# Regrouping the tiled matmuls of a fused attention and gating layer: v pairs and head sums in five clusters, a fourth product buffer, and two output groups in one sequence

## The chip, the cores and the metric

The kernel runs on one core of a Trainium2 chip. The core has five engines, each with its own in-order stream of instructions: TensorE (PE in the profile; its weight loads are listed as PEld), VectorE (DVE), ScalarE (ACT), GpSimd (POOL) and SyncE (SP), and they wait for each other through semaphores. Matrix products go to an accumulator memory (PSUM) of eight banks, and VectorE or ScalarE carries them on from there. DMA queues are issued from SP, ACT and POOL. The metric is the device time of one execution in microseconds (us), the median of the runs taken.

## What is computed

From one input x (2048 tokens, 512 features) a layer norm is taken, and two branches work on it; the output is x plus both.

```python
xn = _layernorm(x)
# attention: 32 heads of 16, each token looks at itself and 7 earlier ones, 2 apart
qkv = xn @ wqkv
logits = einsum('bhsd,bhswd->bhsw', q, k_gathered) * 16 ** -0.5      # w = 0..7
o = einsum('bhsw,bhswd->bhsd', softmax(logits), v_gathered)
att = o @ wo
# gating: F = 1376, two halves of 688
z = gelu(xn @ w_in)
z1, z2 = z[..., :688], layernorm(z[..., 688:])
g = einsum('ts,bsf->btf', w_sp, z2) + b_sp
out = x + att + (z1 * g) @ w_out
```

All inputs and the output are in bfloat16; sums are kept in float32.

## The kernel before

The 2048 tokens are 16 tiles of 128, and for attention two halves (`th`) of 1024. Two hand-written lists set the order. `ten` is the order of the steps that hang on TensorE, `vec` of those that hang on VectorE. Every step has a short name; `needs` says which steps must have been written down before it, and `advance` writes both lists out into one program, in which each engine keeps its own order. What waits at run time follows from the data: a step waits until what it reads is there and what it overwrites has been read.

The steps that matter here:

- `z`*i* and `h`*i*: the second half of w_in for token tile *i* (eight full matmuls, L203), and its gelu on ScalarE (L209); `q`*i*: the sum of squares on ScalarE (L214). `zs`*i*: the mean and variance for four tiles, three small VectorE operations (L220 to L222) and the root on GpSimd (L223, L224). `zn`*i*: the normalisation of one tile on VectorE (L230), which waits for that root.
- `y`*i*: the first half of w_in for a tile (L203 again, gelu L235). `k`*b c*: q or k for 512 tokens, two chunks of features (L243, copied by ScalarE, L245).
- `v`*n*: a "v pair", v for two of the 16 places in a head (L258). Its matmuls use a quarter of the array's columns each, at tile positions (0, 0) to (0, 96), four side by side.
- `m`*th w*: the products of q and k for two window places on VectorE (L278, two operations of 128x4096), into one of the product buffers. Their features are added up in two folds, the first on VectorE (`f`, L281) or by an accumulating DMA from the GpSimd queue (`d`, L287), the second on VectorE (`p`, L282).
- `S`*th w*: the head sum (L293), four column-tiled matmuls against a matrix of ones, and the scaled copy of the result by ScalarE into `a_sb` (L295). It needs `p`*th w*.
- `M`*j*: a tile of the token mixing (L362, 32 full matmuls), which reads all of z2, so that its *k*-th pair of matmuls needs `zn`*k*. `g`*j*: the gate on VectorE (L370) and the transposes of the result. `x`, `e`, `u`, `i`, `c`: the softmax. `a`*th.n*: the weighted sum of v on VectorE (L335, L339, L348).
- `B`: a small transpose of the bias on TensorE (L576). `W`, `O`, `X`: loads. `O` loads wo and w_out over the weights that were there.
- `Q`*n*: an output group of four token tiles: attention @ wo (L412, row-tiled, four matmuls of 32 rows side by side), the full feature blocks of the gating branch (L400) and its remainder of 48 rows (L406, two side by side). `F`*n* adds the residual on VectorE (L417) and stores.

A product buffer is a "home". Before, there are three: two tiles of their own, and the first part of the buffer of z1. `home` gives the home of each of the eight products; a product that takes a home again waits for the head sum that read it last.

PSUM is held in three tiles of two banks (`mm`) and two of one bank (`aux`), each taken in turn. In the output stage all eight banks are dealt out to the groups (`banks`, `po`).

Three sizes of matmul tile occur in the regrouped part: 128*128 (full), 128*32 (v pairs, head sums) and, in the output groups, 64*128 for the remainder (48 rows in use) and 32*128 for attention. The source calls going from one to another a change of kind. Output groups 0 and 1 before: full, remainder, attention, then attention, remainder, full.

Of the kernel before, what the change touches and what calls it, by code (L numbers as in the profile page):

```python
# [14 lines left out]
S = 2048  # L15
D = 512
NT = S // P
# [21 lines left out]
def kernel(  # L39
# [45 lines left out]
    xnT = xnT_r[:].rearrange("p (c s) -> p c s", c=C)  # L85
    op = xnT_r[:].rearrange("p (t d s) -> p t d s", t=2, d=DH)
    wts = sb.tile([P, C * (3 * D + F)], BF16, name="wts")
    w_q, w_k, w_v = [wts[:, n * C * D:(n + 1) * C * D].rearrange("p (k f) -> p k f", k=C) for n in range(3)]
    w_z = [wts[:, C * (3 * D + n * FH):C * (3 * D + (n + 1) * FH)].rearrange("p (k f) -> p k f", k=C) for n in range(2)]
    wo_r = wts[:, 0:DH * D].rearrange("p (d n) -> p d n", d=DH)  # L90
    wout = wts[:, DH * D:(DH + MF + 1) * D].rearrange("p (m n) -> p m n", m=MF + 1)
    qk_r = [sb.tile([P, QKH], BF16, name=f"qk{t}") for t in range(2)]
# [7 lines left out]
    z1_r = sb.tile([P, NT * FP], BF16, name="z1")  # L100
    z1u = z1_r[:].rearrange("p (i f) -> p i f", i=NT)
    prod.append(z1_r[:, 0:2 * C * HS])
    xs = z1_r[:, 0:NT * D].rearrange("p (i d) -> p i d", i=NT)
    xn = [z1_r[:, NT * D + n * D:NT * D + (n + 1) * D] for n in range(8)]
    vp = sb.tile([P, DH, 2, HALO + GS], BF16, name="vp")
# [8 lines left out]
    def nxt(kind, pool):  # L114
        t = pool[count[kind] % len(pool)]
        count[kind] += 1
        return t
# [145 lines left out]
        G.dma_start(vp[H:P, :, :, 0:HALO], vp[0:P - H, :, :, GS:GS + HALO])  # L263
        G.dma_start(vp[0:H, :, 1, 0:HALO], vp[P - H:P, :, 0, GS:GS + HALO])

    home = {(0, 0): 0, (0, 1): 1, (0, 2): 2, (0, 3): 0, (1, 0): 1, (1, 1): 0, (1, 2): 1, (1, 3): 0}

    def prod_ops(th, w2):
        pr = prod[home[th, w2]].rearrange("p (w c s) -> p w c s", w=2, c=C)
# [18 lines left out]

    def head_sum(th, w2):
        pr = prod[home[th, w2]].rearrange("p (w c s) -> p w c s", w=2, c=C)  # L290
        pl = nxt("aux", aux)
        for g in range(4):
            PE.matmul(pl[32 * g:32 * g + 32, :], rsel[:], pr[:, :, 0, g * GS:(g + 1) * GS],  # L293
                      start=True, stop=True, tile_position=(0, 32 * g))
        A.activation(a_sb[:, th, 2 * w2:2 * w2 + 2, :], pl[:].rearrange("p (w s) -> p w s", w=2),  # L295
                     ACT.Copy, scale=float(DH) ** -0.5)

    def softmax_max(th):
# [125 lines left out]
    for i in range(5, NT):  # L424
# [1 line left out]
    front += " n15 t15"  # L426
    vec = front.split() + """
        zs0 LW m00 j00 zn0 zn1 zn2 zn3 f00 p00 K m01 d01 m02 d02 zs4 m03 d03 zn4 zn5 zn6 zn7
        zs8 p01 p02 zn8 zn9 zn10 zn11 m10 p03 W1 f10 zs12 p10 zn12 zn13 zn14 zn15
        m11 d11 g0 x0 m12 d12 p11 g1 u0 m13 p12 W2 W3 f13 p13 c0 g2  # L430
        a0.0 a0.1 g3 x1 a0.2 a0.3 g4 a0.4 g5 a0.5 a0.6 a0.7 g6 u1 a0.8 g7 a0.9 g8 a0.10 g9 a0.11 c1 g10
        a1.0 a1.1 g11 a1.2 a1.3 g12 a1.4 g13 a1.5 g14 a1.6 a1.7 g15 a1.8 a1.9 F0 a1.10 a1.11 F1 F2
    """.split()
    ten = """
        T0 T1 GL z0 z1 h0 T3 h1 z2 h2 z3 h3 k00 k01 q0 k02 k03 q1 q2 q3 k10 k12 k11 k13
        W0 k20 z4 h4 q4 k21 z5 h5 q5 k22 z6 h6 q6 k23 z7 h7 q7 k30 z8 h8 q8 k31 z9 h9 q9 S00
        k32 z10 h10 q10 k33 z11 h11 q11 z12 h12 z13 h13 q12 v0 q13 v1 S01 S02 z14 h14 z15 h15 q14 v2 q15 v3 B
        y0 v4 S03 y1 M0 S10 v5 v6 EL v7 H e0 M1 EG y2 S11 y3 y4 EL1 i0 EG1 M2 y5 y6 y7 y8 S12 S13 M3 y9 y10 y11 M4 y12
        M5 W4 W5 y13 y14 y15 EL2 e1 M6 M7 W6 i1 M8 M9 W7 M10 O4 M11 O0 M12 O1 M13 O2 M14 O3 X0 M15 X1 Q0 Q1 Q2 Q3
    """.split()  # L440
    prods = [n for n in vec if n[0] == "m"]

    def needs(n):
        k, a = n[0], n[1:]
        i = int(a) if a.isdigit() else 0
        if k == "T":
            return [f"n{i}"]
        if k == "z" and a.isdigit():
            return [[f"T{i}"], ["T1", "n2"], ["z1"], ["T3"]][i] if i < 4 else [f"t{i}"]
        if n == "GL":  # L450
            return ["T1"]
        if k == "q":
            return [f"h{i}"]
        if k == "h":
            return [f"z{i}"]
        if k == "k":
            last = 4 * int(a[0]) + 3
            return [f"T{last}" if last < 4 else f"t{last}"]
        if k == "v":
            return ["t15", "LW"]  # L460
        if k == "S":
            return ["p" + a]
        if k == "m":
            b = 2 * int(a[0])
            r = ([f"k{x}3" for x in (b, b + 1)] + ["K"]) if b else ["k03", "k12"] + (["k13"] if a != "00" else [])
            prev = [p for p in prods[:prods.index(n)] if home[int(p[1]), int(p[2])] == home[int(a[0]), int(a[1])]]
            return r + (["S" + prev[-1][1:]] if prev else [])
        if k == "j":
            return ["k13"]
        if k in "fdp":  # L470
            return ["m" + a]
        if k == "K":
            return ["k13"]
        if n[:2] == "zs":
            return [f"q{int(n[2:]) + x}" for x in range(4)]
        if k == "x":
            return [f"S{a}{w}" for w in range(4)]
        if k in "euic":
            return ["xeui"["euic".index(k)] + a]
        if k == "a":  # L480
            r = ["c" + a[0], "H", "S12"] + (["S13"] if a not in ("0.0", "0.1") else [])
            return r + ([f"y{x}" for x in range(NT)] if a[2:] == "11" else [])
        if k == "H":
            return [f"v{x}" for x in range(8)] + ["d12"]
        if k == "M":
            return [f"zn{x}" for x in range(NT)] + [f"W{i // 2}", "B"] + ([f"g{i - 3}"] if i >= 3 else [])
        if k == "g":
            return [f"M{i}", f"y{i}"]
        if k == "W":
            return [f"M{2 * i - 5}"] if i >= 3 else ["t15"]  # L490
        if k == "y":
            return [f"t{NT - 1}", "LW", "S02"]
        if k == "B":
            return ["LW"]
        if k == "O":
            return [f"y{x}" for x in range(NT)]
        if k == "Q":
            return [["a0.11", "g7", "O4"], ["g7"], ["a1.11", "g15", "F0"], ["F2"]][i]
        if k == "F":
            return [f"Q{i}", f"X{i // 2}"]  # L500
        if k == "X":
            return ["M11" if i == 0 else "M13"]
        return []


    banks = [mm[0][:, 0, :], mm[0][:, 1, :], mm[1][:, 0, :], mm[1][:, 1, :],
             mm[2][:, 0, :], aux[0][:], mm[2][:, 1, :], aux[1][:]]
    groups = [[8 * th + 2 * g + t for g in range(4)] for th in range(2) for t in range(2)]
    po = {i: banks[4 * (n % 2) + g] for n, tiles in enumerate(groups) for g, i in enumerate(tiles)}

    def out_group(n):

# [36 lines left out]
    def do(n):  # L549
# [28 lines left out]
        elif k == "y":  # L578
            z1_tile(i)
        elif k == "M":  # L580
            gates[i] = mix_tile(i)
        elif k == "W":
            load_wsp(i)
        elif k == "O":
            load_wo(i) if i < 4 else load_wout()
        elif k == "X":
            load_res(i)
        elif n == "GL":
            A.preload_act_table(ACT.Gelu_apprx_tanh)
        elif n[:2] == "EG":  # L590
            A.preload_act_table(ACT.Gelu_apprx_tanh)
        elif n[:2] == "EL":
            A.preload_act_table_set("natural_log_exp_and_others")
        elif k == "Q":
            out_group(i) if i < 3 else out_last(i)
# [100 lines left out]
```

## Time and profile before

| what | us |
|---|---|
| three runs | 203.06, 205.81, 211.87 |
| median of the runs | 205.81 |
| the profiled execution | 203.68 |
| its span, first to last instruction | 202.0 |

The profile shows each instruction with its start (us from the beginning of the span), its length, its engine and its source line. Matmuls overlap in the array, so the distance from one start to the next tells more of their cost than their length. A timeline row gathers neighbouring instructions of one kind (x8 is eight of them). Where a row has a bracket, its engine sat idle that long before it, and what is named behind the arrow ended the wait.

### The profile page before, as it was taken

How to read it: one execution, taken by the hardware profiler on the slowest of the kernel's cores; microseconds unless marked ns; L12 is line 12 of the kernel's file. 1: busy time of each engine (PE TensorE's matmuls, PEld its weight loads, DVE VectorE, ACT ScalarE, POOL GpSimd, SP SyncE). 2: the span in 40 equal slices, each digit the busy share in tenths (PEclk: the TensorE clock that was granted, in tenths of full speed). 3: DMA queues.
4: the chain of work that ended last, by engine and by line, in shares of the span. 5: the costliest groups of instructions: out<-in, count | busy, mean ns of one | idle time of the engine just before them, and what ended most of it. 6: DMA issues, size and time to landing. Idle time of an engine off the chain costs nothing.

```text
span 202.0 us, 3839 instructions
## 1 busy us (share of the span) xinstructions
PE 195.9 (97%) x1585; PEld 118.0 (58%) x1585; DVE 176.3 (87%) x193; ACT 95.8 (47%) x149; POOL 37.7 (19%) x62
## 2 busy tenths in 40 slices
PE   7799999999999999999999999999999999999993
PEld 2455555555666666666666666666666664444652
DVE  5779899998799799999999899989989999996233
ACT  3587979999997449796263184311122110000000
POOL 2366682249700431500000000000000000000000
PEclk9999999999999999999999999999999999999999
DMA  5996639999952748976977092786999999402023
GB/s 157 349 271 124 93 87 222 181 151 209 209 112 58 153 91 159 186 84 140 209 168 152 0 240 45 61 198 138 246 209 196 196 309 249 115 28 104 3 104 104
DMA packets 63761, 30.84 MB, mean 153 GB/s; under 512 B 53424, under 2 KB 61984, under 8 KB 63616
## 3 DMA queue, kind: packets, MB, share of 16 engines
q1 hardware_dynamic: 60592, 20.90, 49.9%
q0 software_dynamic: 1904, 6.59, 18.0%
q10 hardware_dynamic: 1248, 3.11, 7.0%
q8 instruction: 12, 0.20, 0.4%
q14 instruction: 5, 0.04, 0.1%
HBM read 10.03 MB, written 2.10 MB: 60 GB/s over the span
## 4 chain that ended last, share of the span: by engine, by line
PE 95%; DMA 3%; SPq 0%; DVE 0%; issue 0%
PE mm L362 37%; PE mm L203 19%; PE mm L243 14%; PE mm L258 7%; PE mm L400 7%; PE mm L412 5%; DMA wts<-in_B_w_in_dram 3%; PE aux L400 2%; PE mm L534 1%; PE aux L293 1%; PE mm L406 1%; PE aux L534 0%; SPq L140 0%; PE aux L191 0%; DVE z L417 0%
## 5 line engine op out<-in xcount | busy, mean ns | idle before, releaser
L362 PE MATMUL mm<-z,wsp 128*128 128x344 bf16 x512 | 75.8, 309 | 0.0
L362 PEld LDWEIGHTS <-wsp 128*128 128x128 bf16 x512 | 49.9, 98 | 25.2 <-issue 0.8
L203 PE MATMUL mm<-wts,xnT 128*128 128x344 bf16 x256 | 40.7, 309 | 1.3 <-DMA wts<-in_B_w_in_dram 1.3
L365 ACT ACTIVATE qk<-mm,b_col 128x688 bf16<-128x688 f32 x16 | 13.3, 833 | 51.7 <-PE mm L362 46.4
L335 DVE TENSOR_TENSOR prod<-vp,a_sb 128x4096 bf16<-128x4096 bf16 x16 | 36.1, 2285 | 0.0
L203 PEld LDWEIGHTS <-xnT 128*128 128x128 bf16 x256 | 24.5, 98 | 15.3 <-issue 2.1
L278 DVE TENSOR_TENSOR prod<-qk 128x4096 bf16<-128x4096 bf16 (+1 forms) x16 | 31.6, 2020 | 0.0
L243 PE MATMUL mm<-xnT,wts 128*128 128x512 bf16 x128 | 29.0, 379 | 0.0
L339 DVE TENSOR_TENSOR prod<-prod,prod 128x8192 bf16<-128x8192 bf16 x6 | 26.5, 4421 | 0.1
L243 PEld LDWEIGHTS <-wts 128*128 128x128 bf16 x128 | 14.4, 113 | 12.3 <-issue 0.2
L245 ACT CAST qk<-mm 128x1024 bf16<-128x1024 f32 x16 | 16.0, 1011 | 3.6 <-PE mm L243 3.6
L417 DVE TENSOR_TENSOR z<-mm,wsp 128x512 bf16<-128x512 f32 (+1 forms) x13 | 8.1, 665 | 8.7 <-PE mm L412 5.5
L258 PE MATMUL mm<-xnT,wts 128*32 128x512 bf16 x256 | 14.7, 382 | 0.0
L400 PE MATMUL mm<-wts,qk 128*128 128x512 bf16 (+1 forms) x65 | 14.7, 371 | 0.0
L235 ACT ACTIVATE z<-mm 128x688 bf16<-128x688 f32 x16 | 11.8, 744 | 4.6 <-PE mm L203 4.6
L172 DVE BATCH_NORM_STATS2 stats<-z 128x6 f32<-128x512 bf16 x16 | 11.0, 685 | 3.2 <-DMA z<-in_A_x_dram 3.1
L400 PEld LDWEIGHTS <-qk 128*128 128x128 bf16 x85 | 8.2, 98 | 9.2 <-issue 0.6
L214 ACT ACTIVATE z_junk<-z 128x688 bf16<-128x688 bf16 x16 | 12.4, 777 | 0.3
L209 ACT ACTIVATE z<-mm 128x688 bf16<-128x688 f32 x16 | 11.9, 746 | 1.4 <-PE mm L203 1.2
L258 PEld LDWEIGHTS <-wts 128*32 128x32 bf16 x256 | 9.3, 140 | 4.7 <-issue 0.9
L370 DVE TENSOR_TENSOR z<-qk,z 128x688 bf16<-128x688 bf16 x16 | 8.2, 513 | 3.4 <-ACT qk L365 3.4
L412 PE MATMUL mm<-wts,xnT 32*128 32x512 bf16 x160 | 10.7, 375 | 0.0
(86 smaller groups left out, 176.5 us busy)
## 6 DMA issues: line engine op xcount, KB each, us to landing
prod<-prod POOLq DMA_DIRECT2D x8, 512.0 KB, 6.9
wts<-in_A_wo_dram ACTq DMA_DIRECT2D x4, 512.0 KB, 6.1
wsp<-in_A_x_dram SPq DMA_DIRECT2D x2, 1024.0 KB, 10.4
out_dram<-z SPq DMA_DIRECT2D x15, 128.0 KB, 1.7
z<-in_A_x_dram SPq DMA_DIRECT2D x3, 512.0 KB, 5.3
wts<-in_A_wqkv_dram SPq DMA_DIRECT2D x2, 512.0 KB, 6.2
z<-z POOLq DMA_DIRECT2D x2, 512.0 KB, 9.7
wts<-in_B_w_in_dram SPq DMA_DIRECT2D x1, 688.0 KB, 5.7
```

The lines of the kernel that those rows point to most:

```text
L203: PE.matmul(pz[:, hh, 0:FHALF], xnT[:, kc, i * P:(i + 1) * P], w_z[part][:, kc, hh * FHALF:(hh + 1) * FHALF], start=(kc == 0), stop=(kc == ...
L214: A.activation(z2_junk[:], z2[:, i, :], ACT.Square, accum_out=zsq[:, i:i + 1])
L243: PE.matmul(pq[:, cc, :], w_c[:, kc], xnT[:, kc, t0:t0 + D], start=(kc == 0), stop=(kc == C - 1))
L245: A.copy(qk[b // 2][:, a, 2 * c2:2 * c2 + 2, o:o + D], pq[:])
L258: PE.matmul(pv[32 * g:32 * g + 32, dd, :], w, r, start=(kc == 0), stop=(kc == C - 1), tile_position=(0, 32 * g))
L278: ops.append(lambda ww=ww, k=k, c=c: V.tensor_tensor(pr[:, ww, c], q[:, c], k[:, c], ALU.mult))
L335: return lambda: V.tensor_tensor(dst, vp[:, :, th, off:off + GS], a_sb[:, th, w].unsqueeze(1).broadcast_to([P, DH, GS]), ALU.mult)
L339: return lambda: V.tensor_tensor(dst, dst, x, ALU.add)
L362: PE.matmul(pg[:, hh, 0:FHALF], w[:, k, (j % 2) * P:(j % 2 + 1) * P], z2[:, k, hh * FHALF:(hh + 1) * FHALF], start=(k == 0), stop=(k == NT ...
L365: A.activation(g.rearrange("p (a b) -> p a b", a=2), pg[:, :, 0:FHALF], ACT.Identity, bias=b_col[:, j:j + 1])
L400: PE.matmul(po[:, cols], uT[th][:, m, t0:t0 + P], wout[:, m, cols], start=(start and m == 0), stop=(stop and m == MF - 1))
L412: PE.matmul(pos[g], op[32 * g:32 * g + 32, th, d, s * P:(s + 1) * P], wo_r[32 * g:32 * g + 32, d, :], start=(start and d == 0), stop=(stop ...
```

## The change

Four things are changed together.

The order on TensorE: v0 goes behind S00, v2 behind S02, v3 and v4 stand together with B and S03, and y0 goes behind S03. S11 moves from between y2 and y3 to stand before S12 and S13, and y9 goes ahead of all three.

The order on VectorE: p01 and p02 go ahead of zs8, and m10 goes ahead of zn8 to zn11.

A fourth home: the product (1, 3) is made in the weight buffer, over the weights of q, k and v and a part of those of z2, which are no longer needed then. The weights are laid out anew, so that those of z1, still in use, lie outside. The head sum of this product goes to a bank of an `mm` tile instead of `aux`.

The output: groups 0 and 1 are written as one sequence, full (0), remainder (0), remainder (1), attention (0), attention (1), full (1); the banks are dealt out in another order.

```diff
-    w_q, w_k, w_v = [wts[:, n * C * D:(n + 1) * C * D].rearrange("p (k f) -> p k f", k=C) for n in range(3)]
-    w_z = [wts[:, C * (3 * D + n * FH):C * (3 * D + (n + 1) * FH)].rearrange("p (k f) -> p k f", k=C) for n in range(2)]
+    w_q, w_k, w_v = [wts[:, C * (FH + n * D):C * (FH + (n + 1) * D)].rearrange("p (k f) -> p k f", k=C) for n in range(3)]
+    w_z = [wts[:, o:o + C * FH].rearrange("p (k f) -> p k f", k=C) for o in (0, C * (FH + 3 * D))]
...
+    prod.append(wts[:, C * FH:C * (FH + 4 * D)])
...
-    home = {(0, 0): 0, (0, 1): 1, (0, 2): 2, (0, 3): 0, (1, 0): 1, (1, 1): 0, (1, 2): 1, (1, 3): 0}
+    home = {(0, 0): 0, (0, 1): 1, (0, 2): 2, (0, 3): 0, (1, 0): 1, (1, 1): 0, (1, 2): 1, (1, 3): 3}
...
-        pl = nxt("aux", aux)
+
+        pl = nxt("mm", mm)[:, 0, :] if (th, w2) == (1, 3) else nxt("aux", aux)[:]
...
-        zs8 p01 p02 zn8 zn9 zn10 zn11 m10 p03 W1 f10 zs12 p10 zn12 zn13 zn14 zn15
+        p01 p02 zs8 m10 zn8 zn9 zn10 zn11 p03 W1 f10 zs12 p10 zn12 zn13 zn14 zn15
...
-        W0 k20 z4 h4 q4 k21 z5 h5 q5 k22 z6 h6 q6 k23 z7 h7 q7 k30 z8 h8 q8 k31 z9 h9 q9 S00
-        k32 z10 h10 q10 k33 z11 h11 q11 z12 h12 z13 h13 q12 v0 q13 v1 S01 S02 z14 h14 z15 h15 q14 v2 q15 v3 B
-        y0 v4 S03 y1 M0 S10 v5 v6 EL v7 H e0 M1 EG y2 S11 y3 y4 EL1 i0 EG1 M2 y5 y6 y7 y8 S12 S13 M3 y9 y10 y11 M4 y12
-        M5 W4 W5 y13 y14 y15 EL2 e1 M6 M7 W6 i1 M8 M9 W7 M10 O4 M11 O0 M12 O1 M13 O2 M14 O3 X0 M15 X1 Q0 Q1 Q2 Q3
+        W0 k20 z4 h4 q4 k21 z5 h5 q5 k22 z6 h6 q6 k23 z7 h7 q7 k30 z8 h8 q8 k31 z9 h9 q9 S00 v0
+        k32 z10 h10 q10 k33 z11 h11 q11 z12 h12 z13 h13 q12 v1 S01 S02 v2 z14 h14 q13 z15 h15 q14 v3
+        q15 v4 B S03 y0 y1 M0 S10 v5 v6 EL v7 H e0 M1 EG y2 y3 y4 EL1 i0 EG1 M2 y5 y6 y7 y8 y9 S11 S12 S13 M3 y10 y11 M4 y12
+        M5 W4 W5 y13 y14 y15 EL2 e1 M6 M7 W6 i1 M8 M9 W7 M10 O4 M11 O0 M12 O1 M13 O2 M14 O3 X0 M15 X1 Q0 Q2 Q3
...
-            return r + (["S" + prev[-1][1:]] if prev else [])
+            return r + (["S" + prev[-1][1:]] if prev else []) + (["v7", "z15"] if a == "13" else [])
...
-            return [f"y{x}" for x in range(NT)]
+            return [f"y{x}" for x in range(NT)] + ["S13"]
...
-    banks = [mm[0][:, 0, :], mm[0][:, 1, :], mm[1][:, 0, :], mm[1][:, 1, :],
-             mm[2][:, 0, :], aux[0][:], mm[2][:, 1, :], aux[1][:]]
+    banks = [mm[1][:, 0, :], mm[1][:, 1, :], mm[2][:, 0, :], mm[2][:, 1, :],
+             mm[0][:, 0, :], aux[0][:], mm[0][:, 1, :], aux[1][:]]
...
+    def out_pair():
+
+        first, second = groups[0], groups[1]
+        for i in first:
+            gated_full(i, po[i], True, False)
+        gated_rest(first, False, False)
+        gated_rest(second, True, False)
+        attention_out(0, 0, [po[i] for i in first], False, True)
+        attention_out(0, 1, [po[i] for i in second], False, False)
+        for i in second:
+            gated_full(i, po[i], False, True)
+
     def out_group(n):
-
         tiles = groups[n]
-        if n % 2:
-            attention_out(n // 2, n % 2, [po[i] for i in tiles], True, False)
-            gated_rest(tiles, False, False)
         for i in tiles:
-            gated_full(i, po[i], n % 2 == 0, n % 2 == 1)
-        if n % 2 == 0:
-            gated_rest(tiles, False, False)
-            attention_out(n // 2, n % 2, [po[i] for i in tiles], False, True)
+            gated_full(i, po[i], True, False)
+        gated_rest(tiles, False, False)
+        attention_out(n // 2, n % 2, [po[i] for i in tiles], False, True)
```

More of the change, by code (lines that the diff above doesn't have):

```diff
@@ L290, in head_sum @@
         pr = prod[home[th, w2]].rearrange("p (w c s) -> p w c s", w=2, c=C)
-        pl = nxt("aux", aux)
+        pl = nxt("mm", mm)[:, 0, :] if (th, w2) == (1, 3) else nxt("aux", aux)[:]
         for g in range(4):
-            PE.matmul(pl[32 * g:32 * g + 32, :], rsel[:], pr[:, :, 0, g * GS:(g + 1) * GS],
+            PE.matmul(pl[32 * g:32 * g + 32], rsel[:], pr[:, :, 0, g * GS:(g + 1) * GS],
                       start=True, stop=True, tile_position=(0, 32 * g))
-        A.activation(a_sb[:, th, 2 * w2:2 * w2 + 2, :], pl[:].rearrange("p (w s) -> p w s", w=2),
+        A.activation(a_sb[:, th, 2 * w2:2 * w2 + 2, :], pl.rearrange("p (w s) -> p w s", w=2),
                      ACT.Copy, scale=float(DH) ** -0.5)
@@ L499, in needs @@
         if k == "F":
-            return [f"Q{i}", f"X{i // 2}"]
+            return [f"Q{[0, 0, 2][i]}", f"X{i // 2}"]
         if k == "X":
@@ L594, in do @@
         elif k == "Q":
-            out_group(i) if i < 3 else out_last(i)
+            [out_pair, None, lambda: out_group(2), lambda: out_last(3)][i]()
         elif k == "F":
```

## Prediction

> **What bounds the kernel now.** I read the profile's busy times first, then the chain of work that ended last, then the timeline of TensorE, and last those of VectorE and GpSimd around the moved steps.
>
> ```profile
> PE 195.9 (97%) x1585; PEld 118.0 (58%) x1585; DVE 176.3 (87%) x193; ACT 95.8 (47%) x149; POOL 37.7 (19%) x62
> ```
>
> ```profile
> PE 95%; DMA 3%; SPq 0%; DVE 0%; issue 0%
> ```
>
> The chain is TensorE (PE) nearly throughout, so a microsecond taken out of its stream is a microsecond off the end, and one of another engine counts only where TensorE comes to wait for it. VectorE is busy for 87%, so such waits are near. The change reorders TensorE's stream; I need its rows from the first head sum (L293) on. Columns: start, length, engine, line, operation, output and input, shape, count.
>
> ```profile
> 43.90 0.40 PE L293 MATMUL aux<-prod,rsel 128*32 128x512 bf16 x4
> 44.23 1.92 PE L243 MATMUL mm<-xnT,wts 128*128 128x512 bf16 x8
> 45.98 1.33 PE L203 MATMUL mm<-wts,xnT 128*128 128x344 bf16 x8
> 47.15 1.89 PE L243 MATMUL mm<-xnT,wts 128*128 128x512 bf16 x8
> 48.87 3.66 PE L203 MATMUL mm<-wts,xnT 128*128 128x344 bf16 x24
> 52.47 3.68 PE L258 MATMUL mm<-xnT,wts 128*32 128x512 bf16 x64
> 55.97 0.39 PE L293 MATMUL aux<-prod,rsel 128*32 128x512 bf16 x4
> 56.19 0.39 PE L293 MATMUL aux<-z,rsel 128*32 128x512 bf16 x4
> 56.51 2.51 PE L203 MATMUL mm<-wts,xnT 128*128 128x344 bf16 x16
> 58.95 3.68 PE L258 MATMUL mm<-xnT,wts 128*32 128x512 bf16 x64
> 62.56 0.18 PE L576 MATMUL aux<-ident,b 16*128 16x16 bf16 x1
> 62.67 1.34 PE L203 MATMUL mm<-wts,xnT 128*128 128x344 bf16 x8
> 63.95 1.96 PE L258 MATMUL mm<-xnT,wts 128*32 128x512 bf16 x32
> 65.73 0.39 PE L293 MATMUL aux<-prod,rsel 128*32 128x512 bf16 x4
> 66.05 1.34 PE L203 MATMUL mm<-wts,xnT 128*128 128x344 bf16 x8
> ```
>
> Starts are what to read here, since lengths overlap. Eight full matmuls of 344 columns take 1.17 us (45.98 to 47.15, so 0.146 each), eight of 512 take 1.72 (47.15 to 48.87, 0.215 each). Four column-tiled ones run side by side in one such slot: from the head sum at 55.97 to the next at 56.19 are 0.22. A v pair (32 matmuls, 8 slots) is then worth 1.72.
>
> **The price of a change of kind.** Between the sizes 128*128 and 128*32 the rows hold more than their matmuls: 56.51 to 58.95 is 2.44 for 16 × 0.146 = 2.34, so 0.10 before a v pair; the v pairs from 52.47 to 55.97 take 3.50 for 3.44, 0.06 more at their beginning; 65.73 to 66.05 is 0.32 for 0.215, so 0.11 on the way out. In going in, a head sum pays about 0.10, a v pair 0.16; between v pair and head sum there is nothing (55.97 to 56.19 shows the slot alone).
>
> **Front half.** Counted up to S03, the changes before are nine: z to S00, S00 to k, z to v0, S02 to z, z to v2, v3 to B, B to y0, y0 to v4, S03 to y1. After, v0 stands in S00's cluster, v2 follows S02, and v3 v4 B S03 stand together: z to S00, v0 to k, z to v1, v2 to z, z to v3, v4 to B, B to S03, S03 to y0. That is eight. B, a matmul of a third kind, now has tiled work on both sides, which takes back one of the two that the lost cluster had. Gone is y0 to v4: 1.28 − 1.17 + 0.06 = 0.17. Moving S11 from between y2 and y3 to S12 and S13 removes one way in and one way out, 0.10 + 0.11 = 0.21. Together −0.38.
>
> **Output groups.**
>
> ```profile
> 164.93 4.48 PE L400 MATMUL mm<-wts,qk 128*128 128x512 bf16 x20
> 169.34 0.61 PE L406 MATMUL mm<-wts,qk 48*128 48x512 bf16 x4
> 169.88 3.84 PE L412 MATMUL mm<-wts,xnT 32*128 32x512 bf16 x65
> ...
> 177.44 1.25 PE L400 MATMUL mm<-wts,qk 128*128 128x512 bf16 x5
> ```
>
> Four remainder matmuls (L406) go two at a time: 2 slots, 0.43, in 0.54. From 169.88 to 177.44 are 7.56 us: 128 attention matmuls in 32 slots (6.88), the second remainder (0.43), and two changes, 0.25. In the new order both remainders stand together, and attention is followed by the full matmuls at once: one change of four goes, −0.12. Sum of the tile changes: −0.38 − 0.12 = −0.50.
>
> In a sentence of its own: the Trainium skill (TensorEngine Tiling, Key Properties) says that changing the tiling mode drains the array, and TensorE: Matmul & The Clock Gate (Single matmul latency) has a constant of 398 cycles at 2.4 GHz, 0.166 us; an estimate from these would be −0.66 for four changes, where the rows have 0.10 to 0.17 each.
>
> **What the new order on VectorE costs.** VectorE's list changes too: before, it runs zs8 p01 p02 zn8–11 m10 p03; after, p01 p02 zs8 m10 zn8–11 p03. So p03 now stands behind a statistics round, m10 and the normalisations, and S03, which needs p03, comes earlier on TensorE.
>
> ```profile
> 54.75 1.23 DVE L282 TENSOR_TENSOR z<-z 128x2048 bf16<-128x2048 bf16 x1 [1.06 <-DMA z<-z]
> 55.89 1.57 DVE L230 TENSOR_SCALAR z<-z,zmean,zrstd 128x688 bf16<-128x688 bf16 x4
> 57.36 4.50 DVE L278 TENSOR_TENSOR prod<-qk 128x4096 bf16<-128x4096 bf16 x2
> 61.76 1.23 DVE L282 TENSOR_TENSOR prod<-prod 128x2048 bf16<-128x2048 bf16 x1
> ...
> 68.06 1.57 DVE L230 TENSOR_SCALAR z<-z,zmean,zrstd 128x688 bf16<-128x688 bf16 x4 [1.18 <-POOL zrstd L224]
> ```
>
> These are p02 (held by its fold transfer), zn8–11, m10, p03, zn12–15. The same pattern as the new one, statistics followed by a long product and only then the normalisation, stands in the old kernel at zs4 m03 zn4:
>
> ```profile
> 44.31 0.16 DVE L220 TENSOR_SCALAR zmean<-zsum 128x4 f32<-128x4 f32 x1
> ...
> 44.85 4.49 DVE L278 TENSOR_TENSOR prod<-qk 128x4096 bf16<-128x4096 bf16 x2
> 50.27 1.66 DVE L230 TENSOR_SCALAR z<-z,zmean,zrstd 128x688 bf16<-128x688 bf16 x4 [0.93 <-POOL zrstd L224]
> ```
>
> ```profile
> 45.60 1.59 POOL L223 TENSOR_SCALAR zvar<-zvar 128x4 f32<-128x4 f32 x1
> 47.28 2.96 POOL L224 TENSOR_TENSOR zrstd<-zvar,mhalf 128x4 f32<-128x4 f32 x1
> ...
> 53.83 1.03 POOL L224 TENSOR_TENSOR zrstd<-zvar,mhalf 128x4 f32<-128x4 f32 x1
> ```
>
> GpSimd's root (L224) takes 1.03 us with VectorE idle and 2.96 beside m03. The two products, 2.20 each, begin at 44.85 and 47.05 and give way at 49.25. L223 ends at 47.19, 0.14 past the first boundary, and L224 at 50.24, 0.99 past the second: each seems to do its work only when the running product is over. So I take the root after m10 to end 0.99 past its second product, and not 1.03 after its own start.
>
> In a sentence of its own: the Trainium skill (SBUF — State Buffer, Who interferes with whom) says that a tensor_tensor with both inputs in SBUF holds the port that GpSimd reads through, and that the one who comes later blocks for the whole instruction; the two ends just worked out agree with that.
>
> Now the clocks. TensorE: S00 43.90, v0 behind it, so k32 stands 1.72 later than at 44.23, and v1 begins at 52.47 + 1.72 = 54.19; S01 is at 54.19 + 0.06 + 1.72 = 55.97, S02 at 56.19 (both where they were), v2 to 58.12, 0.11, z14 z15 to 60.67, v3 v4 3.50 and 0.11, B 0.11 (62.56 to 62.67): S03 at 64.39. VectorE: p02 hands on at 55.89, still held by the transfer; zs8 0.54 (44.31 to 44.85); m10 at 56.43. It must follow S01, whose buffer it takes; S01 is over at 55.97 + 0.39 = 56.36, just in time. Its products give way at 58.63 and 60.83, the root is done at 61.82, zn8–11 run from 61.85 for 1.47 (55.89 to 57.36), p03 from 63.32 to 64.55. S03 waits 0.16 and some hand-over: I take 0.2. Bounds: nothing, if the root ends before m10 does (p03 over at 63.53), and 1.3, if the whole root runs behind m10 (the third rival below).
>
> Behind S03: M0 starts at 64.59 + 0.32 + 2 × 1.17 = 67.25 and reads the last zn (zn15) with its 31st matmul, at 67.25 + 30 × 0.146 = 71.63. zn15 ends 1.56 later than at 69.63 (p03's shift), so at 71.19. It holds by 0.4.
>
> ```profile
> 93.88 1.23 DVE L282 TENSOR_TENSOR prod<-prod 128x2048 bf16<-128x2048 bf16 x1
> ```
>
> ```profile
> 95.54 0.62 PE L293 MATMUL aux<-prod,rsel 128*32 128x512 bf16 x8
> ```
>
> p13 ends at 95.11 and at most 1.56 later, 96.67. S13 now follows y9, S11 and S12: 95.54 + 0.2 − 0.17 − 0.43 (S11 and its changes, gone from ahead) + 1.17 (y9) + 0.43 (two head sums) = 96.74. It just holds. The fourth home spares m13 a wait for S11, which stands at 96.3 now, while m13 comes three products ahead of p13. VectorE's lateness dies out in its waits for the gates behind.
>
> ```profile
> 180.40 2.29 DVE L348 TENSOR_TENSOR xnT<-prod 128x4096 bf16<-128x4096 bf16 x1
> ```
>
> At the end, the first group's sums wait for 0.43 more of remainder matmuls, less what was won: VectorE's last step for the third group (a1.11, over at 182.69 before) comes about 0.1 later. The attention part that needs it starts at 177.44 + 4.30 + 4.41 + 0.54 = 186.7 before, 186.4 after: 3.6 us of cover. Sharing the S13 bank with the mm tiles shifts which buffer each step takes, not how many are free.
>
> **Sum.** −0.50 + 0.2 = −0.3. The profiled execution took 203.68 (span 202.0 and 1.7 around it), so 203.4. The median of the three runs shown is 205.81, the lowest 203.06: the profiled one is near the lowest, and I forecast an execution like it. What the measurement can tell from no change here is about 2%, 4 us; this is a tenth of it.
>
> **Rivals.** (1) No wait at S03: GpSimd slips in beside m10 and p03 is over at 63.53. For: L224 is a very small operation. Against: the 2.96. It gives 203.68 − 0.50 = 203.2. (2) The joined kinds still cost what they did, because the gaps belong to each v pair's weights and not to the change: v4's 0.06 speaks for a part of it, the bare slot between 55.97 and 56.19 against. Then only the wait is left: 203.9. (3) Slower than before: GpSimd gets neither operation in between the two products of m10. At 1.03 each they end at 60.83 + 2.1 = 62.9, p03 at 65.6, S03 waits 1.3, and the time is 203.68 − 0.50 + 1.3 = 204.5. It decides from a root that ends 0.3 later than I have it (62.1). Against it: at zs4 the first got in at the boundary. (4) The fourth home lies in the weight buffer; were the whole buffer one thing to the waits, y5 and all later y tiles would wait for p13. y5 starts at 95.54 − 0.10 − 4 × 1.17 = 90.8 before, p13 ends at 96.7: some 6 us, 209.5.
>
> ```profile
> 29.03 0.98 POOL L166 DMA_DIRECT2D wts<-in_A_wqkv_dram  x1
> ```
>
> Against it: this load wrote the v weights into the same buffer at 29.03 while the k chunks were read from it until 48.87, so waits go by region.
>
> **Chances.** Forecast 0.58 (203.4); (1) 0.18; (2) 0.08; (3) 0.13; (4) 0.03. The first three lie within 203.2 to 203.9. The range is 202.5 to 206.0: below to the lowest run less the whole gain (203.06 − 0.50), above through (3) and the spread that the runs of an unchanged kernel have (203.06 and 205.81 among them). Only (4) is over 2%; with something not thought of on either side, slower 0.06, faster 0.04, same 0.90.
>
> **What would show it.** Right: head sums and v pairs in five stretches, one L406 row of eight, span near 201.7. A wait of L293 for VectorE between 64.3 and 64.8, with GpSimd's root at about 61.8 and VectorE idle for some 0.9 before zn8. Wrong: no such wait (rival 1), one of over 0.5 (rival 3), gaps of 0.1 left inside the joined clusters (rival 2), waits of L203 for VectorE near 90 (rival 4).

## The result, and the profile after

The changed kernel took 202.9 us (median of 22 runs, 202.21 to 223.94), the kernel before, beside it on the same chip, 203.62 us (22 runs, 202.69 to 214.84). The ratio is 0.997, with a 95% interval from 0.9956 to 0.9983: a gain of 0.2 to 0.4%, well inside the 2% that counted as no change. Forecast were 203.4 us, within 202.5 and 206.0, and no change.

Some executions of either kernel take some per cent longer than the rest; the ratios here leave these out, and as the one profiled in the first measurement was among them (TensorE stood 4.1 us for a load of wo), the profile after is that of an execution without such a wait, of the same kernel measured again as the first experiment. Its span is 201.5 us, against 202.0 before.

Its busy times (engine, us, share of the span, instructions), from the page of the profile:

```profile
PE 194.8 (97%) x1577; PEld 118.1 (59%) x1585; DVE 176.2 (87%) x193; ACT 95.8 (48%) x149; POOL 36.8 (18%) x62
```

and its chain of work that ended last, by engine:

```profile
PE 94%; DMA 3%; issue 0%; SPq 0%; DVE 0%
```

TensorE is the whole of the chain as before. So the place to look is again its timeline, first around the regrouped front. Columns as before: start, length, engine, line, operation, output and input, shape, count. Lines have moved by two or more: the head sum is now L295, a v pair L259, z and y are L204, q and k L244, the mixing L364, B is L585.

```profile
43.91 0.40 PE L295 MATMUL aux<-prod,rsel 128*32 128x512 bf16 x4
44.13 1.90 PE L259 MATMUL mm<-xnT,wts 128*32 128x512 bf16 x32
...
54.21 1.96 PE L259 MATMUL mm<-xnT,wts 128*32 128x512 bf16 x32
55.99 0.39 PE L295 MATMUL aux<-prod,rsel 128*32 128x512 bf16 x4
56.20 0.39 PE L295 MATMUL aux<-z,rsel 128*32 128x512 bf16 x4
56.42 1.90 PE L259 MATMUL mm<-xnT,wts 128*32 128x512 bf16 x32
...
60.69 3.68 PE L259 MATMUL mm<-xnT,wts 128*32 128x512 bf16 x64
64.31 0.18 PE L585 MATMUL aux<-ident,b 16*128 16x16 bf16 x1
64.41 0.40 PE L295 MATMUL aux<-prod,rsel 128*32 128x512 bf16 x4
64.75 2.51 PE L204 MATMUL mm<-wts,xnT 128*128 128x344 bf16 x16
67.09 4.83 PE L364 MATMUL mm<-z,wsp 128*128 128x344 bf16 x32
```

Inside a cluster there is nothing left but the slots: S00 to v0 0.22, S01 to S02 0.21, S02 to v2 0.22. And no row has a bracket: S03 at 64.41 did not wait.

The same view of the same kernel, at S11 to S13 and in the shared output groups (full L402, remainder L408, attention L414):

```profile
90.20 6.00 PE L204 MATMUL mm<-wts,xnT 128*128 128x344 bf16 x40
96.13 0.62 PE L295 MATMUL aux<-prod,rsel 128*32 128x512 bf16 x8
96.57 0.39 PE L295 MATMUL mm<-wts,rsel 128*32 128x512 bf16 x4
96.89 0.32 PE L364 MATMUL mm<-z,wsp 128*128 128x344 bf16 x1
...
164.57 4.48 PE L402 MATMUL mm<-wts,qk 128*128 128x512 bf16 x19
168.98 0.82 PE L408 MATMUL mm<-wts,qk 48*128 48x512 bf16 x5
...
169.95 3.84 PE L414 MATMUL mm<-wts,xnT 32*128 32x512 bf16 x65
...
181.30 4.48 PE L402 MATMUL mm<-wts,qk 128*128 128x512 bf16 x20
```

The marks of the kernel before at M0 and M3 (L362) and at the third output group (L400):

```profile
67.23 4.83 PE L362 MATMUL mm<-z,wsp 128*128 128x344 bf16 x32
...
96.09 4.84 PE L362 MATMUL mm<-z,wsp 128*128 128x344 bf16 x32
...
181.77 4.48 PE L400 MATMUL mm<-wts,qk 128*128 128x512 bf16 x20
```

Read from mark to mark, these starts give the whole account. S00 to M3 (43.91 to 96.89) is 52.98. Before it was 43.90 to 96.09, and y9, 1.17, now lies in this stretch too, so that 53.36 is to be compared. That is −0.38. From the first full matmuls of the output to those of the third group (164.57 to 181.30) is 16.73, before 164.93 to 181.77, 16.84: −0.11. M3 to the output is 67.68, before 68.84 less y9, which is 67.67. Together −0.49, and the span is 0.5 shorter.

What VectorE did meanwhile (p02, the last of zs8, m10, zn8 to zn11, p03), in its timeline of this kernel:

```profile
52.50 1.21 DVE L283 TENSOR_TENSOR z<-z 128x2048 bf16<-128x2048 bf16 x1
...
54.09 0.16 DVE L223 SCALAR_TENSOR_TENSOR zvar<-zsq,zvar 128x4 f32<-128x4 f32 x1
56.43 4.50 DVE L279 TENSOR_TENSOR prod<-qk 128x4096 bf16<-128x4096 bf16 x2 [2.18 <-PE aux L295]
60.84 1.56 DVE L231 TENSOR_SCALAR z<-z,zmean,zrstd 128x688 bf16<-128x688 bf16 x4
62.32 1.22 DVE L283 TENSOR_TENSOR prod<-prod 128x2048 bf16<-128x2048 bf16 x1
```

and GpSimd's two operations for the root, in its own:

```profile
54.34 0.20 POOL L224 TENSOR_SCALAR zvar<-zvar 128x4 f32<-128x4 f32 x1 [2.77 <-DVE zvar L223]
54.63 1.03 POOL L225 TENSOR_TENSOR zrstd<-zvar,mhalf 128x4 f32<-128x4 f32 x1
```

m10 began at 56.43, the very time in the forecast, but for another reason: zs8 had ended at 54.25, and m10 waited 2.18 for S01 to give its buffer free. p02 was not held by its fold transfer, zs8 was over 2.2 us earlier than thought, and the root ran in 0.20 and 1.03 in the time in which VectorE stood. So zn8 followed m10 at once, and p03 was over at 63.54, 0.87 before S03.

### The profile page after: what moved, and what is told of

Its sections match the earlier page's. It is cut to its first block, busy times and chain, and to the rows that moved or that the text cites. A ratio compares the mean times of both kernels' runs of the same rounds, so it can differ in the third digit from the quotient of the medians.

```text
span 208.5 us, 3831 instructions
## 1 busy us (share of the span) xinstructions
PE 198.0 (95%) x1577; PEld 119.2 (57%) x1585; DVE 176.1 (84%) x193; ACT 95.8 (46%) x149; POOL 36.7 (18%) x62
## 4 chain that ended last, share of the span: by engine, by line
PE 88%; DMA 10%; issue 0%; SPq 0%; DVE 0%; ACT 0%
PE mm L364 34%; PE mm L204 18%; PE mm L244 13%; DMA wts<-in_A_wo_dram 7%; PE mm L259 7%; PE mm L414 5%; PE mm L402 4%; DMA wts<-in_B_w_in_dram 3%; PE aux L402 2%; PE aux L414 2%; PE mm L543 1%; PE aux L295 1%; PE mm L408 1%; PE aux L543 0%; SPq L141 0%
## 5 line engine op out<-in xcount | busy, mean ns | idle before, releaser
L364 PE MATMUL mm<-z,wsp 128*128 128x344 bf16 x512 | 75.8, 309 | 0.0
L364 PEld LDWEIGHTS <-wsp 128*128 128x128 bf16 x512 | 49.9, 98 | 25.2 <-issue 0.8
L204 PE MATMUL mm<-wts,xnT 128*128 128x344 bf16 x256 | 40.3, 309 | 0.6 <-DMA wts<-in_B_w_in_dram 0.5
L204 PEld LDWEIGHTS <-xnT 128*128 128x128 bf16 x256 | 24.7, 98 | 14.2 <-issue 0.9
L279 DVE TENSOR_TENSOR prod<-qk 128x4096 bf16<-128x4096 bf16 (+1 forms) x14 | 27.1, 1982 | 2.1 <-PE aux L295 2.1
L244 PE MATMUL mm<-xnT,wts 128*128 128x512 bf16 x123 | 28.5, 379 | 0.2
L244 PEld LDWEIGHTS <-wts 128*128 128x128 bf16 x128 | 14.5, 114 | 12.4 <-issue 0.4
L414 PE MATMUL mm<-wts,xnT 32*128 32x512 bf16 x160 | 13.2, 444 | 4.1 <-DMA wts<-in_A_wo_dram 4.1
L259 PE MATMUL mm<-xnT,wts 128*32 128x512 bf16 x256 | 14.8, 381 | 0.0
L402 PE MATMUL mm<-wts,qk 128*128 128x512 bf16 (+1 forms) x62 | 14.2, 370 | 0.4 <-issue 0.3
L402 PEld LDWEIGHTS <-qk 128*128 128x128 bf16 x85 | 8.2, 98 | 9.2 <-issue 0.6
L414 PEld LDWEIGHTS <-xnT 32*128 32x128 bf16 x192 | 5.7, 104 | 11.6 <-issue 8.0
L259 PEld LDWEIGHTS <-wts 128*32 128x32 bf16 x256 | 9.3, 139 | 4.5 <-issue 0.6
```

What stands on the lines that cost most here:

```text
L204: PE.matmul(pz[:, hh, 0:FHALF], xnT[:, kc, i * P:(i + 1) * P], w_z[part][:, kc, hh * FHALF:(hh + 1) * FHALF], start=(kc == 0), stop=(kc == ...
L244: PE.matmul(pq[:, cc, :], w_c[:, kc], xnT[:, kc, t0:t0 + D], start=(kc == 0), stop=(kc == C - 1))
L259: PE.matmul(pv[32 * g:32 * g + 32, dd, :], w, r, start=(kc == 0), stop=(kc == C - 1), tile_position=(0, 32 * g))
L279: ops.append(lambda ww=ww, k=k, c=c: V.tensor_tensor(pr[:, ww, c], q[:, c], k[:, c], ALU.mult))
L364: PE.matmul(pg[:, hh, 0:FHALF], w[:, k, (j % 2) * P:(j % 2 + 1) * P], z2[:, k, hh * FHALF:(hh + 1) * FHALF], start=(k == 0), stop=(k == NT ...
L402: PE.matmul(po[:, cols], uT[th][:, m, t0:t0 + P], wout[:, m, cols], start=(start and m == 0), stop=(stop and m == MF - 1))
```

## The experiments

Two theories on the size stood against each other. A: the tile changes are worth what the rows said, −0.5, and S03's wait is real but comes only when p02's transfer lands late. B: S03's wait was wrong in itself (GpSimd gets through beside VectorE), or the gain comes from something else in the change, VectorE's order or the loads of the output. Four kernels take the change apart, one presses on S03's wait, two on the price of a change of kind, two on the loads.

**The changed kernel again.** No edit.

> The changed kernel once more, for an execution in which wo lands in time. Theory A (each change of kind between tile sizes costs TensorE 0.10 to 0.17 us, four of them are gone, and no new wait has come): span near 201.5, 0.50 shorter than before's 202.0, and no wait of the head sum S03 (L295) for VectorE. Theory B (the forecast: the same saving, of which S03's wait for p03 takes 0.2 back): span 201.7, with that wait between 64.3 and 64.8, and the root on GpSimd ending near 61.8.

Measured 203.23 against 203.75 us, ratio 0.9973 (0.9937 to 1.0009). Its rows are those above: the tile terms came, the wait did not.

**The front alone.** The kernel before with the new order of TensorE up to y1, and VectorE's new order; S11 stays behind y2.

```diff
-        zs8 p01 p02 zn8 zn9 zn10 zn11 m10 p03 W1 f10 ...
+        p01 p02 zs8 m10 zn8 zn9 zn10 zn11 p03 W1 f10 ...
...
-        ... k31 z9 h9 q9 S00
-        k32 z10 h10 q10 k33 z11 h11 q11 z12 h12 z13 h13 q12 v0 q13 v1 S01 S02 z14 h14 z15 h15 q14 v2 q15 v3 B
-        y0 v4 S03 y1 M0 S10 ...
+        ... k31 z9 h9 q9 S00 v0
+        k32 z10 h10 q10 k33 z11 h11 q11 z12 h12 z13 h13 q12 v1 S01 S02 v2 z14 h14 q13 z15 h15 q14 v3
+        q15 v4 B S03 y0 y1 M0 S10 ...
```

> The front half alone: v0 to S00, v2 to S02, v3 v4 B S03 together, and VectorE's new order; S11, the homes and the output as before. Theory A: one change of kind fewer, 0.17 us, span 201.8. Theory B: 0.17 less 0.2 of waiting at S03, span 202.0.

Measured 204.27 us, ratio 1.0017 (0.9986 to 1.0047). The span of its profile, 201.7, is no proof of the gain: it reached S00 0.54 earlier than the kernel before. From S00 to M0 it took 23.18 (43.36 to 66.54), before 23.33 (43.90 to 67.23): −0.15, near the 0.17 of the term for y0 to v4. But then comes a wait at S11. The rows of S00, M0 and S11 in its TensorE timeline:

```profile
43.36 0.40 PE L293 MATMUL aux<-prod,rsel 128*32 128x512 bf16 x4
...
66.54 4.83 PE L362 MATMUL mm<-z,wsp 128*128 128x344 bf16 x32
...
83.14 0.40 PE L293 MATMUL aux<-prod,rsel 128*32 128x512 bf16 x4 [0.32 <-DVE prod L282]
```

S11 stands and waits for p11. M0 to S11 is 16.60, before 16.21: what the front had won, and 0.24 more, is given back; at the output it is still 0.24 behind (S00 to the first full matmuls 121.27, before 121.03). Counted from S00, p11 is over at 39.73 here (83.09 − 43.36) and was at 39.01 before (82.91 − 43.90). Of these 0.72, 0.54 are there already at f10, the step behind p03 (it starts at 62.91 in both kernels, 19.55 and 19.01 after S00). VectorE's wait of 2.17 for S01 ahead of m10 puts it back against TensorE. The other 0.18 is a gap just before p11, whose fold transfers landed after 7.1 us here and after 5.8 before (medians of two). Without that gap S11 would still be late: p11 was 0.53 ahead of it before (82.91 to 83.44), and S11 0.15 earlier with p11 0.54 later take more than that. The profile after says the same: its y2 starts at 82.04, so that S11 behind it would be due at 83.3, and its p11, which waited 0.28 for its transfer, is over at 83.80. In the changed kernel S11 follows y9, at 96.13, and waits for nothing. The front keeps its 0.15 only because another part of the change moves S11.

**S11 and the fourth home alone.** The kernel before with the weights laid out anew, the product (1, 3) in the fourth home and its head sum in an mm bank.

```diff
-        y0 v4 S03 y1 M0 S10 v5 v6 EL v7 H e0 M1 EG y2 S11 y3 y4 EL1 i0 EG1 M2 y5 y6 y7 y8 S12 S13 M3 y9 y10 y11 ...
+        y0 v4 S03 y1 M0 S10 v5 v6 EL v7 H e0 M1 EG y2 y3 y4 EL1 i0 EG1 M2 y5 y6 y7 y8 y9 S11 S12 S13 M3 y10 y11 ...
```

> S11 moved to S12 and S13, y9 ahead of them, the fourth home and the new layout of the weights alone. Both theories: one way into a tiled stretch and one way out fewer, 0.21 us, span 201.8. A rival (the fourth home in the weight buffer holds the y tiles or VectorE): over 202.0, with a wait of L203 or L278 near 86 to 97.

Measured 203.73 us, ratio 0.9994 (0.9969 to 1.0019). The profiled execution had a wait of 5.8 us for wo in the output, so only rows ahead of that are read:

```profile
89.68 6.00 PE L204 MATMUL mm<-wts,xnT 128*128 128x344 bf16 x40
95.61 0.62 PE L294 MATMUL aux<-prod,rsel 128*32 128x512 bf16 x8
...
96.37 1.92 PE L363 MATMUL mm<-z,wsp 128*128 128x344 bf16 x12
```

S00 was at 43.23 here, so to M3 it is 53.14, before 53.36: −0.22, where 0.21 was forecast. The five y tiles from 89.68 have no bracket: the fourth rival, y tiles that wait for the product in the weight buffer, falls.

**The shared output sequence alone.** The kernel before with groups 0 and 1 as in the change's `out_pair`.

> The shared sequence of output groups 0 and 1 alone. Both theories: one change of kind fewer, 0.12 us, span 201.9, and the rows from the first remainder matmul to the full ones behind attention shorter by that. A rival (VectorE's sums for group 0 come later and hold group 2): a wait of the full matmuls of group 2 for VectorE, span 202.0 or more.

Measured 203.99 us, ratio 1.0021 (0.9987 to 1.0055), with a wait of 1.2 us for wo in the middle of the stage in the profiled execution. A term of 0.11 can't be read from this run, and the ratio doesn't tell it from nothing. It is read from the executions without such a wait, and there it repeats: from the first full matmuls of the output to those of the third group, six with the shared sequence (the profile after and five of the kernels further down) have 16.72 or 16.73, and the two with the old one (the kernel before and the front alone) 16.84.

**VectorE's old order in the changed kernel.**

```diff
-        p01 p02 zs8 m10 zn8 zn9 zn10 zn11 p03 W1 f10 zs12 ...
+        zs8 p01 p02 zn8 zn9 zn10 zn11 m10 p03 W1 f10 zs12 ...
```

> The changed kernel with VectorE's order of before (zs8 p01 p02 zn8-11 m10 p03). Theory A (TensorE's order does the saving, VectorE's only has to keep up): v0 ahead of k32 puts the sum of squares q11 1.7 us later on ScalarE, to about 53.7, so zs8, first in line again, holds p01 and p02 behind it; S02 (L295) then waits 0.3 to 0.6 for p02, and the span is 201.8 to 202.1. Rival (the order on VectorE is indifferent, as p02 waits for its transfer anyway): no wait of L295, 201.5.

Measured 203.59 us, ratio 0.9995 (0.996 to 1.003); again a wait for wo (5.6 us) at the output of the profiled execution. VectorE's rows of it, the end of zs8 and p02:

```profile
53.72 0.16 DVE L223 SCALAR_TENSOR_TENSOR zvar<-zsq,zvar 128x4 f32<-128x4 f32 x1 [0.53 <-ACT z_junk L215]
...
54.94 1.22 DVE L283 TENSOR_TENSOR z<-z 128x2048 bf16<-128x2048 bf16 x1
```

zs8 does stand for ScalarE's sums, and p01 and p02 behind it are late; but S02 came 0.26 after S01 (55.96 to 56.22), where the profile after has 0.21. My expectation of a wait there of 0.3 or more missed; it was 0.05. S00 to M3 is 53.04 (43.88 to 96.92), against 52.98 with the new order and 53.36 before: of the 0.38 in this stretch VectorE's order makes 0.06. The ratio can't tell the two orders apart.

**S01 ahead of v1.** This takes away m10's wait for S01, so that m10 can stand right behind zs8, as the forecast had it.

```diff
-        k32 z10 h10 q10 k33 z11 h11 q11 z12 h12 z13 h13 q12 v1 S01 S02 v2 ...
+        k32 z10 h10 q10 k33 z11 h11 q11 z12 h12 z13 h13 q12 S01 v1 S02 v2 ...
```

> The changed kernel with S01 ahead of v1 instead of behind it, in the same stretch, so that m10 finds its buffer free right behind zs8. The forecast's mechanism (GpSimd's root gets through only when a product of VectorE ends): m10 starts near 54.2 instead of 56.4, the root's second operation takes 1.9 or more instead of 1.03 and ends 1.0 after m10, and VectorE waits about 0.9 before zn8. If the root's length at zs4 had another reason: 1.03 again and no wait. Both: the span stays at 201.5, for p03 is early enough either way.

One run, 203.1 us. p02, m10, zn8 to zn11 and p03 on VectorE:

```profile
54.30 1.23 DVE L283 TENSOR_TENSOR z<-z 128x2048 bf16<-128x2048 bf16 x1 [0.48 <-DMA z<-z]
...
55.98 4.49 DVE L279 TENSOR_TENSOR prod<-qk 128x4096 bf16<-128x4096 bf16 x2
61.41 1.56 DVE L231 TENSOR_SCALAR z<-z,zmean,zrstd 128x688 bf16<-128x688 bf16 x4 [0.93 <-POOL zrstd L225]
62.89 1.22 DVE L283 TENSOR_TENSOR prod<-prod 128x2048 bf16<-128x2048 bf16 x1
```

and the root on GpSimd:

```profile
56.16 2.17 POOL L224 TENSOR_SCALAR zvar<-zvar 128x4 f32<-128x4 f32 x1 [3.34 <-DVE zvar L223]
58.41 2.96 POOL L225 TENSOR_TENSOR zrstd<-zvar,mhalf 128x4 f32<-128x4 f32 x1
```

The pattern is the forecast's to the last figure: the root ends at 61.37, 0.99 past the end of m10's second product (55.98 + 2 × 2.20), and VectorE is idle for 0.93 before zn8. p03 was over at 64.11 and S03 stood at 64.32, with no wait and 0.2 to spare. From m10's start to p03's end is 8.13; from the forecast's m10 at 56.43 that would be 64.56, past S03's time of 64.41. So the first half of theory B falls, and the condition that theory A leaves open has a name: GpSimd's root is held, and S03 can come to wait, when zs8 ends no earlier than m10 can start.

**Six more changes of kind.** In the third output group the last tile's full matmuls are put singly between quarters of the attention part: the same matmuls, six changes more.

```diff
...
+        for part in range(4):
+            if part:
+                m = part + 1
+                PE.matmul(po[last], uT[th][:, m, t0:t0 + P], wout[:, m, :], start=False, stop=False)
+            for d in range(4 * part, 4 * part + 4):
+                for g in range(4):
+                    PE.matmul(po[tiles[g]], op[32 * g:32 * g + 32, th, d, s * P:(s + 1) * P], ...
...
```

> The changed kernel with the fourth tile of output group 2 written in pieces: three of its full matmuls stand between four quarters of attention, which makes six more changes of kind and no other work. Theory A (0.10 to 0.13 us for each change): 0.6 to 0.8 us longer than the changed kernel, all of it between those rows, span 202.1 to 202.3. Rival (a change costs nothing by itself, and the gaps in the rows belong to the first weights of a step): under 0.2 longer.

Measured 203.86 us, ratio 1.0022 (0.9983 to 1.0061), against 0.9973 (0.9937 to 1.0009) for the kernel without them; the intervals overlap, so the rows decide. The span of its profile is 201.5, not the 202.1 or more that was expected, because it reached S00 0.66 earlier (43.25). Its TensorE timeline from the group's start (L540 is attention, L537 the single full matmul, L554 the next group):

```profile
180.64 3.40 PE L402 MATMUL mm<-wts,qk 128*128 128x512 bf16 x15
...
187.54 1.04 PE L540 MATMUL mm<-wts,xnT 32*128 32x512 bf16 x16
188.51 0.39 PE L537 MATMUL mm<-wts,qk 128*128 128x512 bf16 x1
188.83 1.04 PE L540 MATMUL mm<-wts,xnT 32*128 32x512 bf16 x16
189.71 0.38 PE L554 MATMUL mm<-wts,xnT 32*128 32x512 bf16 x1
```

A quarter with its single matmul takes 1.29 (187.54 to 188.83): four slots of 0.215, one more for the full matmul, and 0.22 for the two changes. The group takes 9.07 (180.64 to 189.71), without the edit 8.41 (181.30 to 189.71 in the profile after): +0.66, 0.11 for each of six. So the price is shown by adding changes, and not only read from gaps.

**B behind S03.** The changed kernel left B, a matmul of a third kind, between v4 and S03. Here it goes behind S03, where only one side is tiled.

```diff
-        q15 v4 B S03 y0 y1 M0 S10 v5 v6 ...
+        q15 v4 S03 B y0 y1 M0 S10 v5 v6 ...
```

> The changed kernel with B (the small transpose of the bias) moved from between v4 and S03 to behind S03, so that v3, v4 and S03 stand together and B has tiled work on one side only. By the prices of the changed kernel's own profile one change of kind is gone, 0.11 us: from the start of S00 (43.91 there) to the start of M0 (67.09), 23.18 us there, I expect 23.07, S03 right behind v4 some 0.22 earlier (about 64.2), no wait for p03 (which ended at 63.54), and a span shorter by 0.1 at an equal start. Against the kernel before that is -0.5 to -0.6 us in all, a ratio of 0.997, which the rounds can hardly tell from the changed kernel's 0.9973. Rival: S03, now earlier, stands in front of p03 and waits (if the root on GpSimd is held behind m10, as where S01 was put ahead of v1, p03 ends at 64.1): then M0 starts where it did, 23.18.

Measured 202.98 against 203.5 us, ratio 0.9957 (0.9929 to 0.9985), all 12 runs within 202.55 to 203.77. Its TensorE timeline:

```profile
43.53 0.40 PE L295 MATMUL aux<-prod,rsel 128*32 128x512 bf16 x4
...
60.32 3.68 PE L259 MATMUL mm<-xnT,wts 128*32 128x512 bf16 x64
63.83 0.39 PE L295 MATMUL aux<-prod,rsel 128*32 128x512 bf16 x4
...
66.60 4.83 PE L364 MATMUL mm<-z,wsp 128*128 128x344 bf16 x32
```

S00 to M0 is 23.07, in the changed kernel 23.18: one change of 0.11, and no wait at S03. It is the best of the versions by its ratio, but the intervals overlap: what sets it apart from the changed kernel is shown by the rows, not by the medians. (The other 0.38 of its shorter span, 201.0, lies before S00, at a load of weights.) GpSimd's root shows a third case here:

```profile
56.05 3.19 POOL L225 TENSOR_TENSOR zrstd<-zvar,mhalf 128x4 f32<-128x4 f32 x1
```

It began a moment before m10 (56.06), was held through the first product, and was over at 59.24, during the second: long, and yet free of cost, since zn8 had to wait for m10 anyway. The fold transfer took 9.8 us in this execution and held p02 for 1.56; zs8 ended 0.39 before m10 started, and that was enough.

**The loads of wo earlier.** In three of the executions above, and in the one profiled in the first measurement, TensorE stood in the output stage for a load of wo. Two kernels issue the loads of w_out and wo two mixing tiles earlier, the changed kernel and the one with B moved.

```diff
-        M8 M9 W7 M10 O4 M11 O0 M12 O1 M13 O2 M14 O3 X0 M15 X1 Q0 Q2 Q3
+        M8 O4 M9 O0 W7 M10 O1 M11 O2 M12 O3 M13 M14 X0 M15 X1 Q0 Q2 Q3
```

> The changed kernel with the loads of w_out and wo (O4, O0 to O3) issued two mixing tiles earlier, behind M8 to M12 instead of M10 to M14. Theory C (in some executions the last of wo lands after attention's first matmuls want it, and this alone makes them 2 to 7 us longer, with the clock lowered after the wait): wo has landed by about 163 in each, no wait of L414 for it, span 201.5 in the profile, and the runs over 205 grow fewer. Rival (the long executions have another cause): the same share of long runs. What may go wrong: ScalarE, from whose queue they are issued, waits there and lets TensorE's banks fill.

Measured 203.18 us, ratio 1.0002 (0.9957 to 1.0046). With B moved:

> B behind S03 as in the run beside it, and the loads of w_out and wo issued two mixing tiles earlier. If the long waits of the output stage for wo are what separates this kernel's longer executions from its short ones, none of its executions should show one, the profiled one has no wait of L412 or L414 for a DMA, and the median lies near the fastest executions, about 202.9 (ratio 0.995). If they come from something else, the early loads change nothing: ratio as in the run beside it, and executions over 205 remain.

Measured 202.96 us, ratio 0.9971 (0.9939 to 1.0003). Neither profiled execution had a wait for wo, and neither kernel became faster. Executions over 205 us did not grow fewer in the first: five of 12 (205.15 to 214.53), against three of 12 when the changed kernel was measured again. The second had two (206.53 and 208.35), the kernel with only B moved none. So waits for wo are not the only source of long executions. The second one's profile (206.53 us) shows another, on TensorE at S02 and S03:

```profile
58.95 0.40 PE L295 MATMUL aux<-z,rsel 128*32 128x512 bf16 x4 [2.96 <-DVE z L283]
...
67.53 0.40 PE L295 MATMUL aux<-prod,rsel 128*32 128x512 bf16 x4 [0.41 <-DVE wsp L356]
```

and on VectorE at p02:

```profile
57.67 1.23 DVE L283 TENSOR_TENSOR z<-z 128x2048 bf16<-128x2048 bf16 x1 [3.73 <-DMA z<-z]
```

Here p02 stood 3.73 for its fold transfer, S02 behind it 2.96, the root ran wholly beside m10 (2.17 and 2.96), p03 was over at 67.48, and S03 waited 0.41 (the row behind the arrow is the small operation after p03). It is the forecast's wait, in an execution in which its condition held. Its size is not that of the changed kernel: with B behind it, S03 is due 3.51 after v3's start (60.32 to 63.83 above) instead of 3.72 (60.69 to 64.41), so 0.21 of the wait belongs to this order. No profiled execution of the changed kernel itself shows the wait. The lists of DMA issues (output and input, queue, count, size, median us from issue to landing) of the profile after and of this execution, in the stretch from 44 to 56 us, show the transfer itself:

```profile
z<-z POOLq DMA_DIRECT2D x1, 512.0 KB, 7.4
```

```profile
z<-z POOLq DMA_DIRECT2D x1, 512.0 KB, 12.8
```

## Why the prediction was right

The forecast of no change and its range held, but they would have held under the first three rivals too, and so say little about the mechanism. The terms of the sum say more: all but one came out, and that one made the forecast gain 0.2 too small.

**The tile changes: right in every term.** −0.38 to M3 was forecast and measured, in its two parts too (0.15 for 0.17, 0.22 for 0.21); −0.12 in the output was −0.11. The price of 0.10 to 0.16 a change, read from gaps, held when six were added (0.11 each) and when one more was taken away (0.11). The estimate made beside it from the Trainium skill (TensorEngine Tiling, Key Properties, with the latency constant of TensorE: Matmul & The Clock Gate), −0.66, is too large by a third: the measured −0.49 decides.

**S03's wait: the mis-sized term, +0.2, measured 0.** The step that failed is "p02 hands on at 55.89, still held by the transfer". That the transfer holds p02 was taken from the profile of before, where it landed 10.0 us after its issue, as if it belonged to the kernel. Over the twelve profiled executions of this case it took between 6.9 and 12.8, nine of them under 9, and not shorter with the change than without: in the three executions with VectorE's old order it took 7.0, 7.1 and 8.1, against 10.0 in the profile of before. In the profile after it took 7.4, and the chain behind the step fell with it: zs8 earlier, the root done while m10 waited for S01. What stands behind that step was borne out where its condition held: GpSimd held until a product is over (S01 moved: 0.99 past the second, 0.93 of idle VectorE), and a wait at S03 when p02 is held long enough (0.41, with a transfer of 12.8 and B moved). With 9.8 it was not long enough. S03 came at 64.41 where 64.39 was forecast without the wait; that m10 started at the forecast 56.43 is luck, since another wait, that for S01, set the time.

**The covers held.** No row of M0, of the y tiles or of S11 to S13 has a wait; the third group's attention began at 186.25 (forecast 186.4) and VectorE's a1.11 was over before 182.8 (180.47 and 2.29; forecast 0.1 later than 182.69). S13, which was to hold by 0.07 only, held by 1.0 (p13 over at 95.56, S13 at 96.57), as VectorE was less late than thought. The move of S11 was worth more than the 0.21 of its term: without it S11 waits for p11, and the front's gain is lost. The prediction took the two as independent, and they are not.

**The rivals.** (1), no wait at S03, 203.2, is what came, though not for its reason: GpSimd did not slip in beside m10, it was done before. (2), joined kinds still cost, falls by the slots of 0.21 and 0.22 in the clusters. (3), the root wholly behind m10, did not come in any execution: with S01 moved the first operation got in at the boundary. (4), y tiles that wait, falls.

**How sure the size is.** By the rows the change takes 0.49 off, 0.24% of 203.7; the ratio's interval, 0.17 to 0.44% less, holds this, and leaves out the forecast 0.3 (0.15%) by a hair. Of the parts alone no ratio differs from 1; that they sum as they do rests on the rows. These repeat where nothing waits: from S00 to the first full matmuls of the output the changed kernel took 120.66 and 120.67 in its two profiled executions, with S11 moved alone it took 120.82, and the kernel before and that with the output changed alone, whose fronts are the same, took 121.03 and 121.04.

## What to carry to other kernels

Where a kernel interleaves tiled and full matmuls, count the borders and price one from the starts on either side: here 0.11 us, so that even four of them are a quarter of a per cent of the time, and worth it only if no other engine's step comes due earlier by them. A wait for a DMA that one profile shows is a sample, not a property of the schedule: before a term is built on it, ask what the sum is with the landing time at both ends. And read a change of many parts from mark to mark in the timeline: it settles tenths of a microsecond that no comparison of medians does.

## What was not expected of the hardware

The same accumulating transfer of 512 KB, issued at the same point of GpSimd's stream, landed after 6.9 to 12.8 us in twelve profiled executions; the longest of them held TensorE for 3 us. GpSimd's issue of it took 0.84 us in the execution with 7.4 and in that with 12.8, so the delay arose behind the issue. Loads of wo likewise held it for 1.2 to 5.8 us in four executions and not at all in others. In the two profiled executions with the loads moved (by 9 to 11 us for the first three of wo, by 4.4 for the last) there was no such wait, but there was none either in several without the move, and longer times remained. Which traffic delays either is open; it was not tried.

GpSimd's small tensor_tensor took 1.03 us with VectorE idle, 2.96 when it came after a long VectorE product had begun, 3.19 when its record begins 0.01 before one, and 1.89 in three executions with VectorE's old order, where the shorter p02 ran beside it and VectorE then stood 0.93 before zn8. Behind the long products it was over 0.99 and 0.98 past the end of one. By the Trainium skill (SBUF — State Buffer, Who interferes with whom), who comes later blocks for the whole instruction. The 2.96 agree with that. The 3.19 do not as they stand, since GpSimd was first by its record and was yet the one held; whether 0.01 us between two records can tell who came first is open.
